# Attention with a state-space convolution beside it: exponentials in units of three and two PSUM banks, shift taps as diagonal matmuls, and a planner that charges tiling-mode changes

## Chip, cores, metric

One NeuronCore of a Trainium2 chip. The metric is device time in microseconds (us) of one execution. The kernel before takes 927.62 us (median of 3 runs, 927.57 to 927.8).

## The reference

Two branches share one input `x` (2048 x 640, bf16) and are mixed by a gate:

```python
g = sigmoid((x * gate_w).sum(-1))
# A: shifted k times v, long convolution by FFT, times q
k_shift[t] = sum_j k[t - j] * shift_k[:, j]          # 4 taps a channel
kv = k_shift * v
a = x * (irfft(rfft(kv, 2S) * rfft(ssm_k, 2S))[:S] + kv * ssm_D)
# B: 32 query heads of width 20, one head of keys and values
p = softmax(q @ k.T * 20 ** -0.5)                     # 32 x 2048 x 2048
b = (p @ v) @ wo
out = g * a + (1 - g) * b
```

The softmax needs 32 x 2048 x 2048 exponentials: 2048 tiles of 128 x 512. They set the time; all else is meant to fit beside them. An exponential here is one ACTIVATE, ScalarE's instruction, over two or three banks of PSUM (these kernels keep one tile in a bank).

## The kernel before

A Python planner (a list scheduler with a cost for each instruction) fixes the order of every engine when the program is built. Score matmuls put up to four tiles, one per 32-row group of the array (in the trace the four start 3 ns apart, and the page gives them 0.40 us together, at 301.77 us), into a ring of three pairs of PSUM banks; ScalarE takes the exponential of a pair; values matmuls (PV) add the result up in bank 6. Bank 7 serves everything else. Twice in each of the last 27 of 32 query groups VectorE computes the exponential of a pair in ScalarE's place.

```python
def pairs(u): return (2 * u) % 3, (2 * u + 1) % 3          # ring of three pairs of banks

def EXP(u, h):                                             # a pair of banks: 128 x 1024
    p = pairs(u)[h]; slot = (2 * u + h) % 5
    if h == 1 and on_dve(u): return DEXP(u, p)             # VectorE reads the ring's pair
    op("act", ... e.activation(ET[slot], ps[:, 1024 * p:1024 * p + 1024], Exp, scale=SCALE), cost 0.904)

for u in range(lo, hi):
    EXP(u, 0)
    QK(u + 1, (0, 1) if split else (0, 1, 2, 3))           # scores: 0.03 us a tile, the last 0.27
    EXP(u, 1)
    PV(u - 1)
    if split: QK(u + 1, (2, 3))                            # after VectorE has read the pair
...
# planner, TensorE: another matmul may go ahead of the next score round
if mm.ready <= t and mm.cost <= gap + SLACK: return mm     # SLACK = 0.2 us
# and a matmul of zeros, if TensorE was busy less than FILL = 0.5 of the last 2.4 us
...
# kshift: 16 slabs of overlapping K rows, on VectorE
tt(pd, ks, w4, mult, 2560); tt(sm, pd[0:2], pd[2:4], add, 1280); tt(sm0, sm0, sm1, add, 640); tt(kv_i, sm0, vs, mult, 640)
```

Of the kernel before, what the change touches and what calls it, by code (L numbers as in the profile page):

```python
# [18 lines left out]
FILL = 0.5  # L19


class Op:
    __slots__ = ("eng", "fn", "deps", "cost", "kind", "name", "prio", "grp", "alts", "port", "nbytes", "main",
                 "cont", "nun", "succ", "ready", "start", "end", "placed", "sig", "value", "lane", "known", "seq",
                 "banks", "last", "floating", "tail", "attached", "lat", "iss")

    def __init__(self, eng, fn, cost, kind, name, prio):
# [30 lines left out]
        self.iss = 0.35  # L58


class Group:


    def __init__(self, banks, prio, name):
        self.banks = banks
        self.prio = prio
        self.name = name
        self.bank = None
        self.mms = []
        self.evacs = []  # L70
        self.pos = 0
        self.nun = 0
        self.ready = 0.0
# [62 lines left out]
class Scheduler:  # L136


    def __init__(self, graph, bank_free=(0, 1, 2, 3, 4, 5, 6, 7)):
# [16 lines left out]
        self.active = []  # L156

# [9 lines left out]
    def run(self):  # L167
# [21 lines left out]
        while left:  # L189
            e = min(ENGS, key=lambda x: self.t[x])  # L190
            op = self.pick(e, self.t[e])
            if op is None:
                self.t[e] += 0.04
                guard += 1
                if guard > 400000:
                    missing = [(o.name, o.eng) for o in g.all if not o.placed][:20]
                    raise RuntimeError("the schedule does not end: %s" % missing)
                continue
            guard = 0
            self.place(op, e)  # L200
            if op.name != "fill":
                left -= 1
# [38 lines left out]
    def pick_pe(self, t):  # L241
# [4 lines left out]
        if self.float_left:  # L246
            f = self.float_left.pop(0)
            return f
        if not (m is not None and m.cont):
# [5 lines left out]
        if m is not None:  # L255
# [5 lines left out]
            if m.nun == 0:  # L261
# [7 lines left out]
                if ok:  # L269
# [3 lines left out]
                    gap = r - t  # L273
        if self.open is not None:
            gr = self.open
            mm = gr.mms[gr.pos]
            if mm.ready <= t and mm.cost <= gap + SLACK:
                return mm
            return None
        best = None  # L280
        for gr in self.gcand:
            if gr.ready <= t and gr.mms[0].cost <= gap + SLACK:
                b = None
                for x in gr.banks:
                    if not self.bank_claimed[x] and not self.bank_busy[x] and self.bank_ready[x] <= t:
# [19 lines left out]
        _, gr, b = best  # L305
        self.gcand.discard(gr)
# [7 lines left out]
    def place(self, op, e):  # L314
        t = self.t[e]
        op.eng = e
        if op.alts:
# [32 lines left out]
        if e == "pe" and op.cost > 0.05:  # L350
            self.active.append((op.end - op.cost * 0.92, op.end))
        if op.name == "pv":
# [4 lines left out]
        if gr is not None:  # L357
            if e == "pe" and op in gr.mms:
                gr.pos += 1
                if gr.pos == len(gr.mms):  # L360
# [20 lines left out]
    def emit(self, nc):  # L381
# [3 lines left out]
        for op in self.linear:  # L385
            drop = [d for d in op.deps if op.eng == "pe" and d.eng == "pe" and d.kind == "c"]
# [77 lines left out]

DVE_J = [()] * 5 + [(2, 9)] * 27
# [8 lines left out]
def c_fast(n):  # L474
    return 0.16 + 0.52e-3 * n

# [13 lines left out]
class Kernel:  # L490

    def __init__(self, nc, aps):
# [6 lines left out]
        self.crow0 = None  # L499

# [13 lines left out]
    def group(self, name, prio, banks=(7,)):  # L514
# [34 lines left out]
    def alloc(self):  # L549
# [33 lines left out]
        for i in range(5):  # L583
            sb(f"ET{i}", [128, 1024], BF16)
# [35 lines left out]
        for i in range(2):  # L620
            early0 += [(f"tprod{i}", [128, 520], I32), (f"tcosp{i}", [128, 520], I32)]
        keep = [("wqst", [128, NDC, D], BF16), ("ksq", [128, NSC, 20], F32)]
        early = [("kslab0", [128, 4, D], BF16), ("kslab1", [128, 4, D], BF16), ("kslab2", [128, 4, D], BF16),
                 ("vslab0", [128, D], BF16), ("vslab1", [128, D], BF16), ("vslab2", [128, D], BF16),
                 ("kprod", [128, 4, D], BF16), ("kshs", [128, 2, D], BF16), ("w4", [128, 4, D], BF16)]
# [18 lines left out]
        self.early_fams = ["kslab", "vslab", "w4"] + [n for n, _, _ in early + keep]  # L644
# [297 lines left out]
    def attention(self, I):  # L942
        T = self.T
        op = self.op
        N = NB * 8 * NSC

        def pairs(u):
            return (2 * u) % 3, (2 * u + 1) % 3

        def QK(u, rs=(0, 1, 2, 3)):  # L950
            Iu, g, j = u // 128, (u // 16) % 8, u % 16
            pa, pb = pairs(u)
            banks = (2 * pa, 2 * pa + 1, 2 * pb, 2 * pb + 1)
            first = None
            for r in rs:
                o = op("pe", lambda e, r=r, Iu=Iu, g=g, j=j, bk=banks[r]: e.matmul(  # L956
                    self.bank(bk), T["kT4"][32 * r:32 * r + 21, 128 * j:128 * j + 128],
                    T[f"qT{Iu % 2}"][32 * r:32 * r + 21, g, :], start=True, stop=True, tile_position=(32 * r, 0)),
                    [("kT4", j // 4), ("qT", Iu % 2, g)], [("ps", banks[r])], 0.03 if r < rs[-1] else 0.27, name="qk",
                    main=True, cont=(r > rs[0]), banks=(banks[r],))  # L960
                if r == rs[0]:
                    first = o
                else:
                    first.deps.update(d for d in o.deps if d.eng != "pe")
                    first.banks = tuple(banks[x] for x in rs)

        def EXP(u, h):
            p = pairs(u)[h]
            slot = (2 * u + h) % 5
            if h == 1 and on_dve(u):  # L970
                return DEXP(u, p)
            op("act", lambda e, p=p, slot=slot: e.activation(  # L972
                T[f"ET{slot}"][:, :], self.ps[:, 1024 * p:1024 * p + 1024], ACT.Exp, scale=SCALE),
                [("ps", 2 * p), ("ps", 2 * p + 1)], [("ET", slot)], 0.904, name="exp", main=True,
                after=self.sins if u == 0 else ())

        def DEXP(u, p):

            par = self.ndexp % 2
            self.ndexp += 1  # L980
            J, E, kJ = T[f"dJ{par}"], T["dE"], ("dJ", par)
            lo = J[:, :].bitcast(dt.uint16).rearrange("p (n t) -> p n t", t=2)[:, :, 0]
            Ef, Jf = E[:, :].bitcast(F32), J[:, :].bitcast(F32)
            k = dict(port=True, name="dexp", prio=-600.0 + 0.01 * u)
            V = self.dve
            V(lambda e, p=p: e.tensor_scalar(J[:, :], self.ps[:, 1024 * p:1024 * p + 1024], SCALE * LOG2E * 65536.0,  # L986
                                             EOFF * 65536.0, ALU.mult, ALU.add),
              [("ps", 2 * p), ("ps", 2 * p + 1)], [kJ], c_ps(1024), prio=-8000.0, name="dexp0")
# [8 lines left out]
        def PVmm(r, j, src, key, late=False, **k):  # L997
            return op("pe", lambda e, r=r, j=j, src=src: e.matmul(  # L998
                self.bank(6)[32 * r:32 * r + 32, :], T["vaug"][:, j, :], src[:, 512 * (r % 2):512 * (r % 2) + 512],
# [3 lines left out]
        def PV(u):  # L1003
            j = u % 16
            rs = (0, 1) if on_dve(u) else (0, 1, 2, 3)
            for r in rs:
                slot = (2 * u + r // 2) % 5
                o = PVmm(r, j, T[f"ET{slot}"], ("ET", slot), cost=0.03 if r < rs[-1] else 0.27, main=True,
                         cont=(r > 0), banks=(6,))
                o.last = j == NSC - 1  # L1010
                if j == 0:
                    self.pv0 = o
                if o.last and r == 0:
                    o.deps.update(self.late_pv)
                    self.late_pv = []
            if on_dve(u):
                a = PVmm(2, j, T["ETd"], "ETd", late=True, cost=0.03, after=[self.pv0])
                b = PVmm(3, j, T["ETd"], "ETd", late=True, cost=0.27)
                a.floating = True
                a.tail = (b,)  # L1020
                b.deps.add(a)
                b.attached = True
                self.late_pv += [a, b]

        def on_dve(u):
            return u % 16 in DVE_J[u // 16]

        lo, hi = I * 128, I * 128 + 128
        if I == 0:
            QK(0)  # L1030
        for u in range(lo, hi):
            if u + 1 < N:
                if (u + 1) % 128 == 0:
                    self.qproj_next(I + 1)
            EXP(u, 0)
            split = on_dve(u)
            if u + 1 < N:

                QK(u + 1, (0, 1) if split else (0, 1, 2, 3))
            EXP(u, 1)  # L1040
            if I == 0 and u == 40:
                self.gate_fin()
            if u > 0:
                PV(u - 1)
                if u % 16 == 0:
                    self.norm((u - 1) // 128, ((u - 1) // 16) % 8)
            if split and u + 1 < N:
                QK(u + 1, (2, 3))
        if hi == N:
            PV(N - 1)  # L1050

# [96 lines left out]
    def kshift(self):  # L1148
        T = self.T
        k, v = self.aps["A_k"][0], self.aps["A_v"][0]  # L1150
        wst = T["kprod"][:, :, :].rearrange("p a b -> p (a b)").rearrange("p (d j) -> p j d", j=4)
        self.dma(T["kprod"][:, :, :].rearrange("p a b -> p (a b)"),
                 self.aps["A_shift_k"].rearrange("d j -> (d j)").partition_broadcast(128), writes=["kprod"],
                 nbytes=655360, prio=3, after=self.crow0)

        for j in range(4):
            self.dve(lambda e, j=j: e.tensor_copy(T["w4"][:, j, :], wst[:, 3 - j, :]), ["kprod"], ["w4"], 0.6,
                     prio=22)
        for idx, i in enumerate(list(range(1, NSC)) + [0]):
            par = idx % 3  # L1160
            ks, vs = T[f"kslab{par}"], T[f"vslab{par}"]
            kk = [("kslab", par, j) for j in range(4)]
            pr = 24.0 + 4.0 * idx
            r0 = 128 * i - 3
            if i == 0:
                self.pool(lambda e, ks=ks: e.memset(ks[0:4, 0:3, :].bitcast(I32), 0), (), kk, 1.2, prio=pr - 10,
# [297 lines left out]
```

## Time and profile before

| kernel before, profiled run | value | how to read it |
|---|---|---|
| span | 928.0 us | first to last instruction; the profiled run took 929.8 us, the timed ones 927.6 |
| ScalarE | 903.9 us busy | 970 exponentials of 128 x 1024 are 890 us of it |
| exponentials | 25.5 to 917.2 us | ends 917 ns apart; anything above that is called lateness here, 2.4 us in all (sums of lateness are good to 0.2 us) |
| TensorE, VectorE | 804.4 and 615.4 us busy | both with room |
| granted TensorE clock | mean 0.983 | see below |

The chain and the costly groups are in the prediction. One line of the page is worth more attention than I gave it: the granted clock by slices of the span, in tenths, and what stretches around three drops hold (columns: stretch, its length, busy us of TensorE with number of matmuls, weight load, VectorE, ScalarE, GpSimd, granted clock, DMA share, GB/s).

```profile
PEclk9999999999999999999999999999999998999898
```

```profile
9.50:12.90 3.40, 1.09 (x29) 0.82 (x30) 0.30 (x2) 1.79 (x4) 0.99 (x2) 0.99 1.02 193
12.90:16.30 3.40, 3.40 (x27) 1.48 (x23) 2.13 (x10) 0.86 (x3) 0.00 (x0) 0.50 0.62 134
115.30:118.70 3.40, 1.51 (x21) 0.47 (x17) 3.40 (x6) 3.40 (x5) 0.00 (x0) 1.00 0.64 215
118.70:122.10 3.40, 3.40 (x17) 0.66 (x17) 3.40 (x8) 3.40 (x5) 0.00 (x0) 0.50 0.53 161
763.80:767.20 3.40, 2.48 (x23) 0.74 (x20) 2.39 (x3) 3.40 (x5) 3.32 (x4) 1.00 0.00 0
767.20:774.00 6.80, 6.74 (x31) 1.41 (x30) 5.78 (x4) 6.66 (x8) 3.39 (x3) 0.50 0.27 72
```

In these three places the clock is halved, for 3.4 us or a multiple of that, after 3.4 us in which TensorE was busy for 1.1 to 2.5 us; full-array matmuls of 512 columns then start 400 to 427 ns apart for 216. Little use alone does not decide it: from 528.3 to 531.7 us of the same trace TensorE was busy for 2.4 us with 22 matmuls, and the clock held.

### The profile page before, as it was taken

To read this page: it belongs to the slowest core of one execution; us is meant where nothing else is said; L and a number is where in the kernel's file an instruction comes from. 1 tells how busy PE (TensorE), PEld (TensorE's weight loads), DVE (VectorE), ACT (ScalarE), POOL (GpSimd) and SP (SyncE) were. 2 spreads that over 40 slices of the span, in tenths; PEclk is the share of its full clock that TensorE was granted. 3 is DMA by queue.
4 is the path that set the end of the run, shared out by engine and by line. 5 is a ranking of instruction groups with operands and counts; after the bars stand their busy time and mean duration, and the time that the engine had idled before them with its cause. 6 is when DMAs were issued, how large, how long until landed. Compare 5 with 4: busy or idle time off the path is not lost.

```text
span 928.0 us, 16257 instructions
## 1 busy us (share of the span) xinstructions
PE 804.4 (87%) x6836; PEld 333.9 (36%) x6836; DVE 615.4 (66%) x808; ACT 903.9 (97%) x994; POOL 390.3 (42%) x331
## 2 busy tenths in 40 slices
PE   6877778888998898999898899889999989888886
PEld 3222113443444333444243344333443433332222
DVE  5667884566776676776677667667657666667554
ACT  5999999999999999999999999999999999999995
POOL 2970001768724258723268325468324872000000
PEclk9999999999999999999999999999999998999898
DMA  7722542001000001000001010000000003021000
GB/s 159 256 77 85 190 130 65 13 9 40 18 19 18 13 16 33 19 19 18 18 14 30 20 53 19 18 13 9 17 19 18 13 13 95 26 69 49 20 13 28
DMA packets 40406, 41.18 MB, mean 44 GB/s; under 512 B 20147, under 2 KB 33581, under 8 KB 40333
## 3 DMA queue, kind: packets, MB, share of 16 engines
q1 hardware_dynamic: 38067, 39.56, 13.9%
q8 instruction: 53, 0.87, 0.4%
q10 hardware_dynamic: 2266, 0.59, 0.3%
q14 instruction: 20, 0.16, 0.1%
HBM read 31.76 MB, written 6.02 MB: 41 GB/s over the span
## 4 chain that ended last, share of the span: by engine, by line
ACT 93%; PE 5%; DMA 1%; SPq 1%; DVE 0%; DVEq 0%; issue 0%
ACT ET L972 93%; PE ps L956 1%; PE ps L1405 1%; PE ps L998 1%; DMA xT<-in_A_q_dram 1%; SPq L671 1%; PE ps L842 0%; PE ps L1318 0%; PE ps L898 0%; PE ps L1116 0%; PE ps L1123 0%; PE ps L1254 0%; DVE outsb L1138 0%; ACT L747 0%; PE ps L856 0%; DVEq L446 0%
## 5 line engine op out<-in xcount | busy, mean ns | idle before, releaser
L972 ACT ACTIVATE ET<-ps 128x1024 bf16<-128x1024 f32 x970 | 890.3, 1213 | 2.4 <-PE ps L956 2.0
L956 PE MATMUL ps<-qT,kT 21*128 21x512 bf16 x2048 | 224.4, 388 | 104.9 <-ACT ET L972 95.5
L1285 POOL TENSOR_TENSOR Pp<-X,K 128x512 f32<-128x512 bf16 x120 | 170.3, 1446 | 276.7 <-DVE K L1273 276.7
L998 PE MATMUL ps<-ET,vaug 128*32 128x512 bf16 x1940 | 210.0, 394 | 1.0 <-ACT ET L972 1.0
L956 PEld LDWEIGHTS ps<-qT,kT 21*128 21x128 bf16 x2048 | 56.2, 91 | 273.0 <-ACT ET L972 266.0
L986 DVE TENSOR_SCALAR dJ<-ps 128x1024 uint32<-128x1024 f32 x54 | 66.1, 1223 | 47.3 <-PE ps L956 47.2
L998 PEld LDWEIGHTS ps<-ET,vaug 128*32 128x32 bf16 x1940 | 52.3, 93 | 116.6 <-issue 112.5
L1285 POOL TENSOR_TENSOR AB<-Pp 128x256 bf16<-128x256 f32 x80 | 84.4, 1055 | 5.9
L991 DVE SCALAR_TENSOR_TENSOR dE<-dJ,dE 128x1024 f32<-128x1024 uint16 x54 | 79.4, 1471 | 0.4
L994 DVE SCALAR_TENSOR_TENSOR ETd<-dJ,dE 128x1024 bf16<-128x1024 f32 x54 | 78.1, 1446 | 0.8
L1318 PE MATMUL ps<-AB,Tcos 128*128 128x256 bf16 x320 | 76.2, 275 | 1.0 <-DVE K L1273 0.9
L993 DVE SCALAR_TENSOR_TENSOR dJ<-dJ 128x1024 f32<-128x1024 uint16 x54 | 75.1, 1391 | 0.8
L1405 PE MATMUL ps<-Tcos,zeros 128*128 128x512 bf16 x213 | 70.8, 409 | 0.0
L1318 PE MATMUL ps<-AB,Tsin 128*128 128x256 bf16 x280 | 67.3, 274 | 0.0
L1285 POOL TENSOR_TENSOR Pp<-Pp 128x512 f32<-128x512 f32 x40 | 61.3, 1532 | 3.1
L1265 DVE TENSOR_SCALAR X<-ps 128x512 bf16<-128x512 f32 x35 | 24.1, 690 | 47.1 <-PE ps L1254 46.9
L1254 PE MATMUL ps<-ssm_kT,Tsin 128*128 128x256 bf16 x320 | 49.5, 274 | 0.0
L1254 PE MATMUL ps<-kv,Tsin 128*128 128x256 bf16 x320 | 48.2, 274 | 0.0
L1254 PE MATMUL ps<-kv,Tcos 128*128 128x256 bf16 x320 | 46.7, 275 | 1.4 <-DVE kv L1181 0.5
L989 DVE TENSOR_SCALAR dE<-dJ 128x1024 uint32<-128x1024 uint32 x54 | 46.4, 860 | 1.2
L898 PE MATMUL ps<-xT,wq_pad 128*128 128x512 bf16 x160 | 44.9, 393 | 1.4 <-DVE qT L545 1.0
L1056 DVE COPY acc<-ps 128x512 f32<-128x512 f32 x31 | 21.4, 691 | 35.9 <-PE ps L998 35.4
(136 smaller groups left out, 736.5 us busy)
## 6 DMA issues: line engine op xcount, KB each, us to landing
kslab<-in_A_k_dram SPq DMA_DIRECT2D x15, 640.0 KB, 3.6
rbc<-scr_d SPq DMA_DIRECT2D x31, 256.0 KB
scr_o<-oTn SPq DMA_DIRECT2D x24, 128.0 KB
xn<-in_A_q_dram SPq DMA_DIRECT2D x4, 640.0 KB
vslab<-in_A_v_dram SPq DMA_DIRECT2D x16, 160.0 KB, 3.6
kst<-in_A_ssm_k_dram SPq DMA_DIRECT2D x5, 512.0 KB
out_dram<-outsb SPq DMA_DIRECT2D x14, 160.0 KB
oTp<-scr_o SPq DMA_DIRECT2D x12, 160.0 KB, 3.2
```

Source lines behind the costliest of these rows:

```text
L956: o = op("pe", lambda e, r=r, Iu=Iu, g=g, j=j, bk=banks[r]: e.matmul(self.bank(bk), T["kT4"][32 * r:32 * r + 21, 128 * j:128 * j + 128], T ...
L972: op("act", lambda e, p=p, slot=slot: e.activation(T[f"ET{slot}"][:, :], self.ps[:, 1024 * p:1024 * p + 1024], ACT.Exp, scale=SCALE), [("p ...
L986: V(lambda e, p=p: e.tensor_scalar(J[:, :], self.ps[:, 1024 * p:1024 * p + 1024], SCALE * LOG2E * 65536.0, EOFF * 65536.0, ALU.mult, ALU.add),
L989: V(lambda e: e.tensor_scalar(E[:, :], J[:, :], 7, 0x7F800000, ALU.logical_shift_left, ALU.bitwise_and), [kJ], ["dE"], c_fast(1024), **k)
L991: V(lambda e: e.scalar_tensor_tensor(Ef, lo, ED, Ef, ALU.add, ALU.mult), [kJ, "dE"], ["dE"], c_ps(1024), **k)
L993: V(lambda e: e.scalar_tensor_tensor(Jf, lo, EP, lo, ALU.add, ALU.mult), [kJ], [kJ], c_ps(1024), **k)
L994: V(lambda e: e.scalar_tensor_tensor(T["ETd"][:, :], Jf, EQ, Ef, ALU.add, ALU.mult), [kJ, "dE"], ["ETd"], c_ps(1024), **k)
L998: return op("pe", lambda e, r=r, j=j, src=src: e.matmul(self.bank(6)[32 * r:32 * r + 32, :], T["vaug"][:, j, :], src[:, 512 * (r % 2):512 ...
L1254: o = self.mm(gr, lambda e, bk, lhs=lhs, rhs=rhs, comp=comp, n=n: e.matmul(self.bank(bk, 256, 256 * comp), lhs, rhs, start=(n == 0), stop= ...
L1285: f = lambda e: e.tensor_tensor(out, a, b, alu)
L1318: self.mm(gr, lambda e, bk, lhs=lhs, fc=fc, comp=comp, h=h: e.matmul(self.bank(bk, 256, 256 * h), lhs, AB[:, fc, :, comp, :], start=(fc == ...
L1405: sch.filler = lambda e: e.matmul(self.bank(6), self.T["zeros"][:, :], self.T["Tcos"][:, 0, 0:512], start=False, stop=False)
```

## The change

Its intent, by its own words: exponentials over three and two banks by turns, so that ScalarE executes fewer instructions; VectorE's tiles in a bank of their own, out of the ring; the four shift taps as matmuls with diagonal matrices; a planner that knows what a change of TensorE's tiling mode costs. In the trace of the kernel before such a change shows as a later start: the values matmuls start 0.314 us after the scores and full-array matmuls 0.322 us after the values, for 0.216 us between full-array matmuls of 512 columns, so some 0.1 us a change (an estimate: these differences are 0.098 and 0.106 us). The core of the diff (cut: memory, names, the riding of VectorE's score tiles, dependencies):

```diff
-FILL = 0.5
+FILL = 0.55
+MODE = {"qk": "r", "dqk": "r", "pv": "c"}
+SWITCH = 0.096
@@ planner
-            if mm.ready <= t and mm.cost <= gap + SLACK:
+            if mm.ready <= t and mm.cost + sw <= gap + SLACK:
+            mode = MODE.get(op.name, "f")
+            if mode != self.mode:
+                t += SWITCH
@@ stream: tiles in order, VectorE's taken out, cut in units of three and two
+            n = 2 if len(self.units) % 2 else 3
+            self.units.append(tiles[i:i + n])
@@ EXP
-            op("act", ... self.ps[:, 1024 * p:1024 * p + 1024] ..., 0.904, ...)
+            lo, w = 512 * base[n % 2], 512 * len(units[n])          # base = (0, 3)
+            op("act", ... self.ps[:, lo:lo + w] ..., c_exp(w), ...) # 0.0633 + 0.8333e-3 * w
@@ DEXP: one 1024-wide read of the ring becomes two of 512 from banks 5 and 7
-            V(... tensor_scalar(J[:, :], self.ps[:, 1024 * p:1024 * p + 1024], ...))
+            gr = self.group("dqk", pr, banks=(5, 7)); gr.rides = True
+            self.evac(gr, "dve", ... tensor_scalar(J[:, 512 * h:512 * h + 512], self.bank(bk), ...))
@@ kshift
-            self.dma(ks[:, :, :], bass.AP(k.tensor, k.offset + r0 * D, [[D, 128], [D, 4], [1, D]]), ...)
-            tt(pd ...); tt(sm ...); tt(sm ...); tt(T["kv"] ...)
+            x = self.g.add("sp", ... e.dma_start_transpose(o, i) ...)
+                        self.mm(gr, ... e.matmul(self.bank(bk, 128, 128 * ii), T["kTr"][:, c, t0:t0 + 128],
+                            T["kdiag"][:, c, j, :], start=(j == 0), stop=(j == 3)) ...)
+                self.evac(gr, "dve", ... e.tensor_tensor(kvp, self.bank(bk)..., kvp, ALU.mult) ...)
```

## The prediction

> **What bounds the kernel now.** I read the page from the top: busy shares, then the chain that ended last, then the costliest groups.
>
> ```profile
> span 928.0 us, 16257 instructions
> ...
> PE 804.4 (87%) x6836; PEld 333.9 (36%) x6836; DVE 615.4 (66%) x808; ACT 903.9 (97%) x994; POOL 390.3 (42%) x331
> ...
> ACT 93%; PE 5%; DMA 1%; SPq 1%; DVE 0%; DVEq 0%; issue 0%
> ...
> L972 ACT ACTIVATE ET<-ps 128x1024 bf16<-128x1024 f32 x970 | 890.3, 1213 | 2.4 <-PE ps L956 2.0
> L956 PE MATMUL ps<-qT,kT 21*128 21x512 bf16 x2048 | 224.4, 388 | 104.9 <-ACT ET L972 95.5
> ...
> L1405 PE MATMUL ps<-Tcos,zeros 128*128 128x512 bf16 x213 | 70.8, 409 | 0.0
> ```
>
> The reader is to see one engine that never rests: ScalarE is busy 97% of the span, the chain lies 93% on its one line L972, and ahead of 970 exponentials it idled 2.4 us in all. The score matmuls (L956) wait for it, not the other way round. TensorE has room[...].
>
> Next, the groups of ScalarE by form, and the view of line L972:
>
> ```profile
> L546 ACT ACTIVATE xT<-ps 128x1024 bf16<-128x1024 bf16 x2 | 2.0, 1020 | 1.2 <-PE ps L814 1.2
> ...
> L546 ACT ACTIVATE xT<-ps 128x512 bf16<-128x512 bf16 x1 | 0.6, 591 | 0.0
> ```
>
> ```profile
> L972 ACT ACTIVATE ET<-ps x970: 1017/1222/1332, 25.5 to 916.1; 128x1024 bf16<-128x1024 f32 x194
> ...
> PE ps L956: 2.0, 4
> ```
>
> From the first: 512 more columns cost 1020 - 591 = 429 ns, 0.838 ns a column. From the second: the exponentials run from 25.5 us to about 917.2 us; 25.5 us lie before them and 10.7 us behind. Their mean of 1213 ns counts queueing: the ends of two neighbouring records lie 917 ns apart (5th and 95th percentile 915 and 918), and 970 x 917 ns = 889.5 us agrees with the 890.3 busy. So one exponential occupies ScalarE for 917 ns, and about 917 - 1024 x 0.8333 = 64 ns of that do not depend on its width.
>
> The timeline at 300 us shows how TensorE answers:
>
> ```profile
> 301.77 0.40 PE L956 MATMUL ps<-qT,kT 21*128 21x512 bf16 x4
> 302.09 0.10 PEld L998 LDWEIGHTS ps<-ET,vaug 128*32 128x32 bf16 x4 [0.23 <-issue]
> 302.09 0.40 PE L998 MATMUL ps<-ET,vaug 128*32 128x512 bf16 x4
> ...
> 302.42 0.83 PE L1254 MATMUL ps<-kv,Tsin 128*128 128x256 bf16 x6
> ```
>
> Four score matmuls start together, the values (PV) matmuls 0.32 us later, the next full-array matmul 0.33 us after that. Full-array matmuls of 512 columns start 0.216 us apart where no mode changes. So a round of up to four tiles costs one stream of 0.216 us, and each change of tiling mode about 0.1 us.
>
> [...] 0.314 us from scores to values and 0.322 us from values to full array, against 0.216 us within a mode. [...] this trace's 128-column transposes start 55 to 56 ns apart (L1200), and I use that for the shift taps.
>
> **The change part by part.**
>
> *Exponentials (on the path).* VectorE keeps 108 of 2048 tiles, as before; 1940 stay on ScalarE, now 388 of three banks and 388 of two, 776 instructions for 970. At 64 ns + 0.8333 ns a column these cost 1344 and 917 ns: 388 x 2.261 = 877.2 us. Against 889.5 us that is **-12.3 us** (194 fixed parts of 64 ns). Nothing else shortens ScalarE's work.
>
> *VectorE's score tiles (off the path, frees a wait).* They leave the ring of six banks and ride along with a score round into banks 5 or 7. Before, 54 times half a round was held back for a 1223 ns VectorE read (L986). After: 108 reads of 512 columns at 0.69 us (as other 128x512 reads from PSUM) = 74.5 us instead of 66.1.
>
> *Shift taps (off the path).* VectorE loses four groups of L1181 (23.9 + 13.5 + 8.0 + 7.7 = 53.1 us) and 2.8 us of weight copies, gains 20 multiplies from PSUM at 0.69 us = 13.8, and one product of 2560 columns, some 2.8 us. With the 8.4 above VectorE comes to about 615 - 31 = 584 us. TensorE gains 320 matmuls x 0.056 = 18 us. K comes in by four DMA transposes in place of overlapping 640 KB slabs; the three transposes of before took 3.4 to 4.9 us each on the queue, and the last taps wait for theirs only after about 18 score rounds, near 45 us, when it should have landed by about 42.
>
> *TensorE.* The instruction order (both kernels build) shows stretches of score rounds rising from 563 to 774 and mode changes from 1631 to 2035; fillers fall from 213 to 142. Estimate: 211 x 0.216 + 404 x 0.1 + 18 - 71 x 0.216 = 46 + 40 + 18 - 15 = +89 us. Adding stretch by stretch from the first score round on, with the durations above, I get 728 us of TensorE occupancy before and 812 us after, against 889 and 877 us of exponentials: 82% and 93%.
>
> *Window.* The chain from one exponential to the one that reuses its banks is 55 ns to the first score matmul, 390 ns for the round, 60 ns to the next ACTIVATE; and since an isolated one takes 1017 ns but adds 917 ns when queued, a round has to end 160 ns before the running exponential's record does. With 917 ns to run, some 310 ns of lateness are free. Before, this held for every full round; now it holds for each three-bank unit's round, and a two-bank unit's has some 740 ns. So the double buffer in five banks is no tighter than the ring of three pairs was.
>
> *Waits.* Before, 12 stretches between score rounds hold more TensorE work than the 1.834 us of their two exponentials, by 1.6 us in all; measured were 12 late exponentials and 2.15 us. After, 68 of 772 overlapping pairs of stretches hold more than the 2.261 us of theirs, by 8.0 us, half of it (each stretch is counted twice) 4.0 us. Scaled by 2.15/1.6 that is 5.4 us of waits, +3.2 us net.
>
> Sum: 927.6 - 12.3 + 3.2 = **918.5 us**; start and tail are taken as they were.
>
> **The rivals.**
> 1. *TensorE becomes a second bound.* For it: 93% occupancy, and nearly half the pairs (346 of 772) filled to 2.22 to 2.24 us of 2.261[...]; 91 score instructions now wait on VectorE inside the in-order stream, 49 before. Against: 142 fillers are left, mostly at the end; VectorE has less to do; before, TensorE waited for VectorE inside the attention for only some 3 us. If the waits grow to 10 to 20 us, the time is 925 to 933 and the gain is gone.
> 2. *The planner's better costs remove waits too.* It now plans the exponential at 0.917 us (0.904 before) and charges mode changes. If the plan is followed, waits stay at 2 us: 915 us, the floor of this change.
> 3. *A start stall*: a K transpose lands late under the V and x loads beside it, and TensorE, in order, stops. Worth 1 to 4 us once: 919 to 922. The margins of 3 us and more speak against it.
> A wider instruction may also lose something at three banks; nothing here tests that width, and 10 ns on each of 388 would be 4 us.
>
> **Range and chances.** 915 is a floor, since ScalarE's work is fixed; below 914 something unforeseen would have to shorten start or tail. Upward the waits are uncertain: 10 us more gives 928. I predict 918.5 us, 8 in 10 between 914.5 and 927. Faster by over 2% needs less than 909.1 us, which no part of the sum offers: 2%. Slower by over 2% needs 31 us of new waits beyond the gain: 4%. Within 2%: 94%.
>
> **What would show it.** Right: exponentials with 776 instructions and 876 to 879 us busy, ends alternately 1344 and 917 ns apart; ScalarE's idle ahead of them 3 to 8 us, released by score matmuls; the first exponential still at about 25.5 us and the last's end 10.7 us before the span's; VectorE near 584 us, TensorE busier with its wait for ScalarE down from 95.5 us. Wrong: idle over 10 us ahead of the exponentials (rival 1, to be seen as score rounds late behind VectorE reads or behind packed full-array work); a fixed part of a three-bank exponential unlike 64 ns; one gap of over a microsecond before 45 us (rival 3); or a longer tail because the convolution ends late.

## The result, and the profile after

918.28 us (median of 4 runs, 917.42 to 918.84) against 927.71 us for the kernel before on the same chip (4 runs, 927.57 to 933.62). Ratios here are the mean time of one kernel's fast runs over that of the other's of the same rounds, so not quite the ratio of the medians: 0.9882, with a 95% interval of 0.9842 to 0.9922.

The page of the changed kernel, the same lines in the same order (the chain by engine stands below the clock):

```profile
span 916.6 us, 16425 instructions
...
PE 862.6 (94%) x7024; PEld 355.5 (39%) x7086; DVE 572.5 (62%) x816; ACT 894.3 (98%) x800; POOL 369.0 (40%) x330
...
PEclk9999999999999999999999999999999999999999
...
ACT 59%; PE 34%; SPq 2%; DVE 2%; DMA 2%; issue 0%; DVEq 0%
...
L1056 ACT ACTIVATE ETA<-ps 128x1536 bf16<-128x1536 f32 x388 | 579.7, 1494 | 3.4 <-PE ps L1024 1.8
L1056 ACT ACTIVATE ETB<-ps 128x1024 bf16<-128x1024 f32 x388 | 417.7, 1077 | 0.0
L1024 PE MATMUL ps<-qT,kT 21*128 21x512 bf16 x2048 | 308.7, 384 | 33.2 <-ACT ETA L1056 16.3
```

776 exponentials for 970, ScalarE 98% busy (97% before), its idle of 3.4 us all ahead of three-bank units. Lateness is more than this idle time: a three-bank exponential that starts after a pause takes 1450 ns, a queued one adds 1343. TensorE is now 94% busy, and the time in which it waits for ScalarE ahead of a score round fell from 95.5 to 28 us (16.3 + 11.6 for the two kinds of unit). The chain runs through TensorE for 34% of the span, before for 5%: two engines are now nearly in step. The clock is whole from 7.7 to 915.7 us, and 0.999 in the mean.

The spans split like this, from the first exponential's start and the last one's end in each trace:

| us | before | after | difference |
|---|---|---|---|
| start, to the first exponential | 25.5 | 24.0 | -1.5 |
| exponentials at their own pace | 889.3 | 877.2 | -12.1 |
| lateness between them | 2.4 | 6.3 | +3.9 |
| tail | 10.8 | 9.2 | -1.6 |
| span (rounded parts) | 928.0 | 916.6 | -11.4 |

By the median spacings alone, with the first exponential counted, the second row is 889.5 and 876.9 us, a difference of -12.6 us; the 0.5 us between the two counts lie in deviations of some nanoseconds and in the longer first exponential.

The timed runs differ by 9.4 us, not 11.4: the profiled run of before was 2.1 us slower than its timed ones, and two of its half-clock stretches lie in the start (12.9 to 16.3 us) and in the tail (917.4 to 920.8 us).

Of the lateness after, 43 of 44 late exponentials (over 30 ns) are units of three banks, whose score round has only the two-bank exponential's 917 ns to run in. Four of them, 1.6 us together, stand behind a late VectorE tile. Timelines of VectorE, and of all engines, of the changed kernel at the first of these:

```profile
446.53 2.24 DVE L1094 SCALAR_TENSOR_TENSOR ETd<-dJ,dE 128x1024 bf16<-128x1024 f32 x1
```

```profile
448.82 0.39 PE L1098 MATMUL ps<-ETd,vaug 128*32 128x512 bf16 x2 [0.62 <-DVE ETd L1094]
...
450.29 1.45 ACT L1056 ACTIVATE ETA<-ps 128x1536 bf16<-128x1536 f32 x1 [0.35 <-PE ps L1024]
```

VectorE's product took 2.24 us (1.44 on average), TensorE stood still for it at its place in the order, and the next three-bank exponential came late. Another, 0.76 us, follows a wait for a K transpose:

```profile
41.75 0.38 PE L1271 MATMUL ps<-kdiag,kTr 128*128 128x128 bf16 x4 [0.58 <-DMA kTr<-in_A_k_dram]
```

The others are small, most of them 30 to 250 ns, and return every 12 or 24 units, where the order of tiles repeats.

### The profile page after: what moved, and what is told of

Read it like the earlier page. It is cut to its first block, busy times and chain, and to the rows that moved or that the text cites. A ratio compares the mean times of both kernels' runs of the same rounds, so it can differ in the third digit from the quotient of the medians.

```text
span 916.6 us, 16425 instructions
## 1 busy us (share of the span) xinstructions
PE 862.6 (94%) x7024; PEld 355.5 (39%) x7086; DVE 572.5 (62%) x816; ACT 894.3 (98%) x800; POOL 369.0 (40%) x330
## 4 chain that ended last, share of the span: by engine, by line
ACT 59%; PE 34%; SPq 2%; DVE 2%; DMA 2%; issue 0%; DVEq 0%
ACT ETA L1056 36%; ACT ETB L1056 23%; PE ps L1024 10%; PE ps L1344 8%; PE ps L1098 7%; PE ps L1408 4%; PE ps L950 2%; SPq L1254 1%; PE ps L1271 1%; DVE ETd L1094 1%; DMA kTr<-in_A_k_dram 1%; PE ps L1188 1%; PE ps L1442 1%; DMA xT<-in_A_q_dram 1%; PE ps L966 1%; SPq L723 1%
## 5 line engine op out<-in xcount | busy, mean ns | idle before, releaser
L1056 ACT ACTIVATE ETA<-ps 128x1536 bf16<-128x1536 f32 x388 | 579.7, 1494 | 3.4 <-PE ps L1024 1.8
L1056 ACT ACTIVATE ETB<-ps 128x1024 bf16<-128x1024 f32 x388 | 417.7, 1077 | 0.0
L1024 PE MATMUL ps<-qT,kT 21*128 21x512 bf16 x2048 | 308.7, 384 | 33.2 <-ACT ETA L1056 16.3
L1098 PE MATMUL ps<-ETB,vaug 128*32 128x512 bf16 x776 | 200.2, 389 | 0.0
L1098 PE MATMUL ps<-ETA,vaug 128*32 128x512 bf16 x1164 | 191.7, 390 | 0.3 <-ACT ETB L1056 0.2
L1024 PEld LDWEIGHTS ps<-qT,kT 21*128 21x128 bf16 x2048 | 76.0, 91 | 215.4 <-ACT ETA L1056 114.8
L1086 DVE TENSOR_SCALAR dJ<-ps 128x512 uint32<-128x512 f32 x108 | 74.1, 686 | 32.7 <-PE ps L1024 32.1
L1098 PEld LDWEIGHTS ps<-ETA,vaug 128*32 128x32 bf16 x1164 | 47.6, 92 | 66.6 <-issue 64.8
L1098 PEld LDWEIGHTS ps<-ETB,vaug 128*32 128x32 bf16 x776 | 48.3, 93 | 47.1 <-issue 46.9
L1344 PE MATMUL ps<-ssm_kT,Tcos 128*128 128x256 bf16 x320 | 53.0, 275 | 0.1
```

Of the source, the lines that this page charges most:

```text
L1024: return e.matmul(self.bank(bk), T["kT4"][32 * r:32 * r + 21, 128 * j:128 * j + 128], T[f"qT{G // 8 % 2}"][32 * r:32 * r + 21, G % 8, :], ...
L1056: op("act", lambda e: e.activation(et(n)[:, 0:w], self.ps[:, lo:lo + w], ACT.Exp, scale=SCALE), [("ps", base[n % 2] + k) for k in range(le ...
L1086: self.evac(gr, "dve", lambda e, bk, h=h: e.tensor_scalar(J[:, 512 * h:512 * h + 512], self.bank(bk), SCALE * LOG2E * 65536.0, EOFF * 6553 ...
L1098: return op("pe", lambda e: e.matmul(self.bank(6)[32 * r:32 * r + 32, :], T["vaug"][:, j, :], src, start=(j == 0), stop=(j == NSC - 1), ti ...
L1344: o = self.mm(gr, lambda e, bk, lhs=lhs, rhs=rhs, comp=comp, n=n: e.matmul(self.bank(bk, 256, 256 * comp), lhs, rhs, start=(n == 0), stop= ...
```

## The experiments

All are correct to the reference. Timed runs come without a trace, so the stretches at half clock are seen only in the profiled run of each; it is told where they were. The record calls a run slow when it lies over 1.5% above the fastest of its kernel; ratios leave slow runs out. The first eight were run on one other chip, in two sets of four, the last four on a third chip, each set beside the kernel before.

| run | median us (range) | ratio to before, 95% interval | lateness in the trace, us | half clock in the trace between 20 us and the tail |
|---|---|---|---|---|
| e1 split | 942.3 (930.1 to 947.0) | 1.0072 (1.0022 to 1.0123) | not used (slow run) | 27.3, 17.1 and 3.4 us |
| e2 taps back | 942.7 (929.7 to 944.0) | 1.0113 (1.0081 to 1.0145) | 16.1, of it 3.0 outside | 37.6 us |
| e3 taps alone | 940.1 (938.6 to 941.6) | 1.0090 (1.0064 to 1.0116) | 14.9 | seven stretches of 3.4 to 10.2 us |
| e4 planner alone | 928.1 (926.9 to 928.8) | 0.9960 (0.9935 to 0.9985) | 2.9 | 3.4 and 3.4 us |
| e5 after again | 921.9 (917.0 to 952.8) | 0.9917 (0.9869 to 0.9964) | 5.6 | none |
| e6 taps and planner | 926.2 (924.2 to 926.5) | 0.9947 (0.9923 to 0.9971) | 0.6 | none |
| e7 split, filled | 933.6 (931.9 to 934.9) | 1.0033 (1.0008 to 1.0057) | 7.9 | none |
| e8 after, filled | 922.9 (918.6 to 927.4) | 0.9918 (0.9886 to 0.9951) | 6.1 | none |
| e9 slack | 921.5 (917.1 to 931.4) | 0.9889 (0.9861 to 0.9916) | 10.2, of it 2.7 outside | 10.2 and 3.4 us |
| e10 early tiles | 915.6 (910.2 to 928.6) | 0.9828 (0.9784 to 0.9872) | 12.8, of it 5.3 outside | 20.5 us |
| e11 both | 910.3 (908.9 to 916.0) | 0.9797 (0.9766 to 0.9829) | 4.5 | none |
| e12 planner blind | 1021.3 (1006.5 to 1028.2) | 1.0930 (1.0872 to 1.0988) | 107 | 44.4 and 37.5 us, late in the span |

The kernel before, in the three sets: 927.3 to 935.6, 926.3 to 934.1 and 927.5 to 933.2 us (11 runs each), where its first three runs had agreed to 0.3 us.

What I overlooked at first: the record has the mean granted clock of every timed run of the experiments, and within one kernel the time follows it. e8 took 918.6 us at 1.000, 920.9 and 921.3 at 0.998, 924.6 and 924.7 at 0.994, 927.4 at 0.989; e5 took 917.0 to 918.8 us at 1.000, 925.1 at 0.990, 929.5 at 0.983 and 952.8 at 0.949. So kernels are best compared at equal clock, and a median far from the full-clock sum is first a matter of the clock.

**e1, the fixed part put back.** Every second three-bank exponential is cut in two ACTIVATEs, so that there are 970 again.

```diff
+            cut = 1024 if n % 4 == 0 else w
+                e.activation(et(n)[:, 0:cut], self.ps[:, lo:lo + cut], ACT.Exp, scale=SCALE)
+                return e.activation(et(n)[:, cut:w], self.ps[:, lo + cut:lo + w], ACT.Exp, scale=SCALE)
```

> The changed kernel with every second three-bank exponential cut into two ACTIVATEs (two banks and one), so that ScalarE again executes 970 of them, as many as before the change; order, banks, taps and planner stay as changed (the planner is told of the 63 ns). Theory (the gain is 194 fixed parts of about 64 ns on ScalarE and nothing else of weight): +194 x 0.064 = +12.4 us on 918.3, less up to 2 us of waits that the longer units absorb: 928.5 to 931 us. Rival A (the gain came from taking VectorE's tiles out of the ring, from the taps or from the planner): the time stays near 918 to 922 us. Rival B (a short ACTIVATE costs no fixed part when it follows at once): 918 to 919 us.

Measured 942.3 us, lowest 930.1. Its profiled run counts as slow and had 47.8 us at half clock. The gain went, as the theory had it, but the median cannot be explained by 12.4 us. The 930.1 us, in the expected range, is the one run at a clock of 0.996; the others had 0.972 to 0.982. e7 repeats it at clocks of 0.995 to 1.000.

**e2, taps back on VectorE.**

```diff
-FILL = 0.55
+FILL = 0.5
@@ kshift, its memory and its keys as in the kernel before
```

> The changed kernel with the shift taps back on VectorE (the old slabs, DMAs and products; FILL back at 0.5 because the plan does not end at 0.55). Theory: VectorE near 611 us busy and TensorE 18 us less, both off the path; the late exponentials of the first 110 us (some 1.5 us, one of them 0.76 us at 44 us) shrink: 916.5 to 919 us. Rival C (part of the gain came from relieving VectorE and the loads): 921 us or more.

Measured 942.7 us: outside the expectation, at clocks of 0.949 to 0.979. The stretch of half clock in its profiled (and fastest) run, against the same stretch of e5, the changed kernel (columns as above):

```profile
110.00:144.40 34.40, 27.91 (x191) 7.72 (x194) 28.26 (x51) 34.40 (x32) 0.89 (x1) 1.00 0.50 160
144.40:182.00 37.60, 37.27 (x185) 11.40 (x184) 11.23 (x17) 26.18 (x23) 0.00 (x0) 0.50 0.12 40
182.00:220.00 38.00, 36.93 (x306) 15.65 (x305) 27.50 (x36) 37.88 (x34) 25.89 (x20) 1.00 0.06 19
```

```profile
110.00:144.40 34.40, 34.19 (x271) 14.60 (x272) 14.36 (x24) 34.38 (x31) 18.92 (x18) 1.00 0.10 29
144.40:182.00 37.60, 36.33 (x299) 15.72 (x301) 17.47 (x28) 37.60 (x34) 22.10 (x20) 1.00 0.06 20
...
```

At half clock TensorE is busy for 37.3 of 37.6 us and gets 185 matmuls done; the changed kernel does 299 in that time at full clock. ScalarE executes 23 instructions for 34: 13.1 us of the 16.1 us of lateness lie in this one stretch. Taken off (an estimate), the run would be at 929.7 - 13.1 = 916.6 us, where the theory put it. What the taps on TensorE did here, if anything, is to fill the stretch before 144 us (34.2 us of TensorE work for 27.9), after which the clock fell in one and not in the other. With FILL changed as well, e2 does not settle which of the two it was.

**e3, taps alone.** The kernel before with the new taps and loads.

```diff
 kshift, its memory, its keys as in the changed kernel; ring of three pairs, bank 7, FILL = 0.5 and all costs as before
```

> The kernel before with the taps on TensorE alone (transposed loads, diagonals; side groups on bank 7 as before). Theory: nothing on ScalarE changes, so 926.5 to 929.5 us, with VectorE some 39 us less busy and TensorE some 18 us more. Rival C (the taps gave part of the gain): 924 us or less.

Measured 940.1 us in a narrow range, 1% slower than before: neither the theory nor its rival. The first late exponential stands behind a load: VectorE waited 3.58 us for V, TensorE 2.79 us for VectorE to clear bank 7.

```profile
38.32 0.69 DVE L1177 TENSOR_TENSOR kv<-ps,kv 128x512 bf16<-128x512 f32 x1 [3.58 <-DMA kv<-in_A_v_dram]
...
39.47 1.06 PE L896 MATMUL ps<-xT,wq_pad 128*128 128x512 bf16 x2 [2.79 <-DVE kv L1177]
```

In that pause the clock fell (38.3 to 45.2 us), and then six times more before the end. 14.9 us of lateness against 2.4 accounts for the slower time. So the taps moved by themselves are a loss, through one wait and the clock; that the work they bring does not count is seen in e6. Why the clock fell the six later times is not shown.

**e4, planner alone.** The kernel before, planned with the new costs.

```diff
+SWITCH = 0.096 (with MODE, and `+ sw` in both tests against the gap)
-0.03 if r < rs[-1] else 0.27
+0.003 if r < rs[-1] else 0.216
-0.904
+0.9166
-FILL = 0.5
+FILL = 0.55
```

> The kernel before with the planner's new costs alone: mode changes at 0.096 us, score and values rounds at 0.216 us, exponential at 0.9166 us, FILL 0.55. Theory: ScalarE's 970 x 917 ns stay, only the 2.4 us of late exponentials can change, by 2 us either way: 925.5 to 929.5 us. Rival D (the planner's knowledge gave the gain): 923 us or less.

Measured 928.1 us, as expected, and ratio 0.9960: 4 us better than before on that chip, because before itself ran at 932 there. The trace has two half-clock stretches of 3.4 us; after each, exponentials are late (1.2 us at 220, 1.3 us at 785 to 788 us).

**e5, the changed kernel again.** No edit.

> The changed kernel itself once more, because the first four experiments showed stretches of half TensorE clock that the two first traces had scarcely (before) or not (after). Theory now: ScalarE's fixed parts give -12.3 us, and on top the time varies[...]. The changed kernel has about 3 windows at or under 0.38 of the array's streaming time, the one before about 10, so the changed one should stay at 917 to 921 us in most executions, with a rare one up to 12 us longer, while before spreads from 927 to 936. Rival: the clock episodes come with the chip, not with the kernel: then both spread alike, the changed one up to 930.

Measured 917.0 to 952.8 us: four of six runs within 917 to 925, one at 929.5, one at 952.8, which is left out of the ratio as slow. The expectation holds for the centre and fails for the slowest run: "up to 12 us longer" was 35. The rival, that both kernels spread alike, is not refuted by the fast runs: the changed kernel's five spread over 12.5 us, up to the 930 that it named, and before over 8 us in the same set. The 952.8 us run had a clock of 0.949, which makes some 97 us at half clock (an estimate: 0.051 x 951 x 2, with 1.0 and 0.5 as the only levels, as in the traces of before and after); where they lay is not known, since it has no trace.

**e6, taps and planner together**, with the old ring: e3 and e4 in one, that is the whole change but the new units and the move of VectorE's tiles out of the ring, which go together.

> Everything of the change but the new exponential units: the kernel before with TensorE taps and the planner's new costs (FILL 0.55). Theory: 970 ACTIVATEs at 917 ns stay the bound: 926 to 930 us, and the half-clock stretches of the taps alone (938 to 942 us) go away, because the planner fills low windows (261 fillers). Rival (the taps on TensorE cost by themselves): 936 us or more. Rival (taps and planner carry the gain together): 922 us or less.

Measured 926.2 us, all six within 2.3 us: the theory. The taps' loss of e3 is gone, and it is as steady as e4. Group of exponentials:

```profile
L980 ACT ACTIVATE ET<-ps 128x1024 bf16<-128x1024 f32 x970 | 889.5, 1271 | 1.1 <-PE ps L964 1.1
```

With 0.6 us of lateness this is the floor of 970 exponentials. At a clock of 1.000, from here (924.2 and 924.4 us) to the changed kernel (917.0, 917.8 and 918.8 us in e5) it is 6.5 us: the new units, net of their lateness (12.6 less some 5 to 6), together with the move of VectorE's tiles. No run parts these two; e7 keeps the move and loses the gain.

**e7, the split with a full clock.**

```diff
 as e1
-FILL = 0.55
+FILL = 0.75
```

> The split of the first experiment (every second three-bank exponential in two ACTIVATEs) with FILL 0.75, which puts 345 fillers into the plan so that the clock should not be halved. Theory: 918.3 + 12.4 less up to 2 = 928.5 to 931 us in nearly every run, at a granted clock of 0.995 or more. Rival (the split itself, not the clock, made 942 us): it stays at 938 us or more with a full clock.

Measured 933.6 us, 931.9 to 934.9; the rival, that the split itself had made the 942 us, is refuted, and the expectation missed by 1 to 4 us. Groups by form:

```profile
L1062 ACT ACTIVATE ETB<-ps 128x1024 bf16<-128x1024 f32 x388 | 426.3, 1099 | 0.0
L1062 ACT ACTIVATE ETA<-ps 128x1536 bf16<-128x1536 f32 x194 | 295.6, 1524 | 0.9 <-PE ps L1024 0.8
L1059 ACT ACTIVATE ETA<-ps 128x1024 bf16<-128x1024 f32 x194 | 207.6, 1070 | 2.1 <-PE ps L1024 0.6 <-PE ps L1104 0.5
L1060 ACT ACTIVATE ETA<-ps 128x512 bf16<-128x512 f32 x194 | 126.0, 649 | 0.0
```

Busy times of neighbouring groups overlap, so I take the spacing of ends: 1343 ns for three banks, 917 for two, 489 for one. They grow by 428 and 426 ns for 512 more columns, 0.836 and 0.832 ns a column. At the 0.8333 ns of the diff's cost (c_exp), which the prediction uses too, each fixed part is 62 to 64 ns at all three widths (1343 - 1280, 917 - 853, 489 - 427). With the first exponential counted, the median spacings add up to 889.1 us, before to 889.5, after to 876.9: 12.2 of the 12.6 us are put back (194 x 63 ns). The timed runs agree: at a clock of 0.998 e7 took 933.6 us twice, and e8, which has the same FILL and no split, 920.9 and 921.3: 12.5 us. Lateness, which I had thought would shrink, is 7.9 us for 6.1 in e8 with the same FILL.

**e8, the changed kernel with more fillers.**

```diff
-FILL = 0.55
+FILL = 0.75
```

> The changed kernel with FILL 0.75 (285 fillers for 142). Theory: the clock is full throughout; the time stays at 916 to 920 us, since fillers go only where TensorE would wait. Rival E (a stream packed this densely is hurt by more fillers): 922 us or more, ScalarE idle over 10 us.

Measured 922.9 us, in the range of rival E; but the profiled run took 918.6 us at full clock with 6.1 us of lateness and under 2 us of ScalarE idle ahead of exponentials, as the theory says and against E's mechanism. The other runs lie 2 to 9 us above it at clocks of 0.998 to 0.989: "the clock is full throughout" failed. Where and why it fell in them stays open.

**e9, half the planner's allowance.**

```diff
-SLACK = 0.2
+SLACK = 0.1
```

> The changed kernel with the planner's SLACK at 0.1 us for 0.2: other matmuls may overrun the next score round's planned start by half as much. The traces of the changed kernel show 44 late exponentials, 43 of them of three banks (whose round has only 917 ns to run), 6 to 6.6 us in all. Theory F (they are the packed stream's overrun): lateness falls to 2 to 4 us and the time at full clock to 914 to 916.5 us. Rival G (they come from VectorE's late ETd and from loads): lateness stays at 5.5 us or more, the time at 917 to 919.

The time (921.5 us) misses the range, again with half-clock stretches in the trace: 46.3 to 56.5 and 568.5 to 571.9 us, which hold 7.5 of 10.2 us of lateness. Outside them 2.7 us are left for the 6.3 and 5.6 of the two traces of the changed kernel, as theory F has it. But the one run of e9 at a clock of 1.000 took 917.1 us, which is G's number, and between e10 and e11, which differ in SLACK only, lateness outside half clock is 5.3 and 4.5 us and the time at 0.999 to 1.000 is 1.2 us apart (means of two and three runs). How much of the lateness is what the planner's own allowance lets other matmuls overrun is therefore not settled.

**e10, VectorE's tiles in the early groups too.** Room for them came from moving the taps.

```diff
-DVE_J = [()] * 5 + [(2, 9)] * 27
+DVE_J = [()] * 1 + [(2, 9)] * 31
```

> The changed kernel with two of VectorE's tile pairs in four of the first five query groups too (16 tiles less for ScalarE), which the taps had kept VectorE from. Theory (ScalarE is the bound): 16 x (427 + 26) ns = -7.2 us: 910 to 912.5 us at full clock. Rival H (TensorE, already filled to 93%, is the bound of the first 150 us): the gain there turns into waits, 915 us or more, ScalarE idle over 10 us.

Three of six runs lie at 910.2 to 912.0 us at clocks of 0.998 to 1.000, as the theory has it; the other three at 919 to 929 (0.974 to 0.987), one of them with the trace: 20.5 us at half clock from 57 us on, and 7.6 us of lateness there.

**e11, both.** e9 and e10 in one.

> Both of the two before together. If both theories hold: 906.5 to 910 us at full clock, 2% below the kernel before; if TensorE has become the bound: 914 us or more.

Measured 910.3 us, 908.9 to 916.0, at the edge of the expected range; 2.0% below the kernel before (interval 1.7 to 2.3%), and the fastest here. The page's head, and the line's view:

```profile
span 907.8 us, 16480 instructions
```

```profile
L1056 ACT ACTIVATE ETA<-ps x385: 1445/1489/1574, 24.2 to 896.7; 128x1536 bf16<-128x1536 f32 x193
L1056 ACT ACTIVATE ETB<-ps x385: 601/1075/1161, 25.5 to 898.0; 128x1024 bf16<-128x1024 f32 x192, 128x512 bf16<-128x512 f32 x1
```

770 exponentials for 776, 7.2 us less at their own pace (868.3 for 875.5), full clock. ScalarE is still the bound.

**e12, the planner blind to mode changes.**

```diff
-SWITCH = 0.096
+SWITCH = 0.0
```

> The changed kernel with SWITCH = 0, so that the planner no longer counts mode changes, all else as changed; it then plans 439 fillers for 142. Theory: some 2000 changes x 0.1 us that the plan leaves out overfill the stretches between score rounds, score rounds come late, ScalarE waits 20 to 60 us: 935 to 975 us at full clock. Rival (the knowledge is not needed, the semaphores sort it out): 917 to 922 us.

Measured 1021.3 us: the direction and the mechanism of the theory, at twice the size. Who ScalarE waited for (us in total, times, longest):

```profile
ACT ETA L1056 <- PE ps L1024: 50.5, 124, 1.4
ACT ETA L1056 <- PE ps L1098: 26.9, 42, 1.6
```

The trace has 1968 mode changes; at the 0.1 us each that was estimated from the trace of the kernel before, some 197 us of TensorE's time are not in this plan, and the planner puts in 439 matmuls of zeros. Of the 107 us of lateness 80 come before 902 us, at full clock; 25 lie in the two stretches at half clock. The semaphores kept the result right (e12 is correct to the reference) and did not keep the order good: it takes 103 us more than the changed kernel.

## Why the prediction was right, and where its steps were not

- **The exponentials' term is shown.** Predicted -12.3 us from 194 fixed parts of 64 ns; the traces give 62 to 64 ns a part at one, two and three banks (at 0.8333 ns a column; e7's spacings give 0.832 and 0.836), and -12.6 us. e7 puts 12.2 us of this back with everything else of the change in place, 12.5 us in time at equal FILL and clock, and e6, which lacks the new units, stays at 924 to 926 us.
- **The lateness term was near in size and wrong in its grounds.** Predicted 5.4 us; 6.3 and 5.6 us measured in two traces at full clock. But I had scaled by before's 2.15 us as if overfull stretches made it. In the trace 2.1 of its 2.4 us come in or just after half-clock stretches (at 119 to 124, 767 to 776, 866 to 875 and 907 to 911 us); 0.4 us is left for overfull stretches, and 0.1 of it, at 102 us, follows an ACTIVATE of the gate (L932). The step "Scaled by 2.15/1.6" therefore rests on a coincidence. What the lateness of the changed kernel consists of was in rival 1: late VectorE tiles (1.6 us), and by my reading a densely filled stream (what e9 and e11 show of it is not of one size).
- **"Start and tail are taken as they were" failed by 3.1 us** in the profiled runs, where before had a half-clock stretch in each. In the timed runs of the first chip the missing part is smaller, about 1 us (an estimate: 9.4 less what the other two terms give). That the sum came within 0.3 us of the measured 918.3 is luck in part: the exponentials gained more than predicted, start and tail too, and lateness cost more.
- **The clock was left out of the sum altogether.** I read the row of granted clock and used the matmuls of zeros as a sign of room only. The planner's part of the change, which I knew only as fewer waits (rival 2), seems to work here: before the change about 10 windows of 3.4 us between 28 and 905 us hold matmuls for 0.38 of the array's streaming time or less, after it about 3, with taps and planner alone about 2, in e3 16 (averaged over the windows' unknown phase; a matmul counts its columns by 0.42 ns, 216 ns for 512 of them, and the share of the array that its row and column groups cover). In the last 3.4 us before each of the 27 half-clock stretches of all traces (those at the very end of a span left out) this share was 0.16 to 0.42; its median is about 0.6. But on the grid of 3.4 us on which the half-clock stretches begin, 69 other stretches at 0.42 or less kept the full clock (15 of them in e2, which had one drop): low use goes before every drop and does not bring one every time. What decides is open. e1 and e7, which differ in FILL only, have some 14 and 1 such windows at 0.38 or less, clocks of 0.972 to 0.996 and 0.995 to 1.000, and lie 9 us apart.
- **Rival 1 (TensorE a second bound) is half right.** It did not eat the gain at full clock, and in e10 and e11 ScalarE can still be relieved. But stretches at half clock cost the kernels with the new units more: in those with the ring they lasted 3.4 to 10.2 us, in these up to 37.6 (e12, overfull, 44), and the one of 37.6 us in e2 holds 13.1 us of lateness, where e4 is late by 1.2 and 1.3 us after its two of 3.4 us. Why they lasted longer is not shown.
- **Rival 2 (better costs remove waits)** is right for the ring (0.6 us in e6) and not for the new units.
- **Rival 3 (a K transpose lands late)** happened at a smaller size: 0.58 us of waiting and a 0.76 us late exponential. I had put the transposes' landing at 42 us from those of the input; on the queue the four, of 655 KB each, took 3.4, 5.0, 4.5 and 4.8 us between the loads of V, the third was waited for, and the fourth landed at 46.1 us.
- The side terms: VectorE 572.5 us (584 predicted), the taps 56 ns apart (56), the product of 2560 columns 2.81 us (2.8), TensorE's wait for ScalarE 28 us instead of 95.5.

## What to carry to other kernels

When one engine sets the time, count its instructions as well as its elements: here 194 fewer fixed parts of 63 ns were worth 12.6 us of ScalarE's time, of which 6.5 us were left in the kernel's (e6 against e5 at equal clock), and the fixed part can be read off by the spacing of ends at two widths (here 917 and 1343 ns, 426 ns for the third bank, so 917 - 2 x 426 = 65 ns). A plan that fills another engine to the brim has to charge what the hardware charges (ignoring 0.1 us a mode change cost some 103 us, about 25 of them at half clock), and it gives back some of the gain as small late steps. Look at the granted clock before trusting a small lateness or a small difference, and compare runs at equal clock: one and the same kernel took 917.0 us at 1.000 and 952.8 us at 0.949 (e5).
